# Gate and up products in four row tiles of TensorE: 27 groups of 32 rows in place of 7 passes of 128

## The chip, the core and the metric

One core of one Trainium2 chip runs the whole program. The metric is device time in microseconds from start to end of an execution, as the median of several executions. The profile is of one execution of the same program.

The engines have short names: PE is TensorE's matmuls, PEld its weight loads, DVE is VectorE, ACT is ScalarE, POOL is GpSimd and SP is SyncE, which issues most DMAs.

## What is computed

The input `x` is 2048 rows of 576. After a layer norm it goes through a linear attention block and through a gated feed-forward block; the output is `x + s * silu(f)`. The part that is changed is the first half of the feed-forward block:

```python
def _B_ref(x, w_gate, w_up, w_down):
    g = jnp.einsum("bsd,df->bsf", x, w_gate)     # 2048x576 by 576x4608
    u = jnp.einsum("bsd,df->bsf", x, w_up)       # 2048x576 by 576x4608
    h = _gelu(g) * u
    return jnp.einsum("bsf,fd->bsd", h, w_down)  # 2048x4608 by 4608x576
...
xn = _layernorm(x, axis=-1)
s = _A_ref(xn, A_wqkv, A_wo)
g = _silu(_B_ref(xn, B_w_gate, B_w_up, B_w_down))
return x + s * g
```

All is fp32.

## The kernel before

**Words.** TensorE's fast fp32 format (`F32R`) keeps fewer bits than fp32. Each operand is therefore cut in two: a high word (ScalarE copies it into the F32R type) and a low word (VectorE subtracts the high word from the source). A product of two operands is high times high plus high times low plus low times high.

**Seven products.** Gate and up are computed by Strassen's scheme in Winograd's form. The reduction of 576 is halved to 288, the 256 columns of a weight group are halved to 128, and blocks of 512 rows of x are taken in pairs. So one matrix (2 x 2 blocks of weights by 2 x 2 blocks of x) takes seven products of 128 by 288 by 512 in place of eight. The weight operands are A11, A12, A22 and the sums S1 to S4; those of x are B11, B21, B22 and the sums T1 to T4. There are 36 matrices, a gate and an up matrix for each of 18 groups of 256 columns (`NG`), and each handles both halves of the rows of x (`s` is 1, then 0), so there are 36 x 7 x 2 = 504 products. The x operands stay in SBUF for the whole stage; in the trace they are `xo_B`, `xo_T` (s = 1) and `xr_B`, `xr_T` (s = 0). The weight words are `wa` and `wb`.

**Passes.** The reduction of 288 is 2 x 128 + 32 rows. With two words on each side a product needs high-high, high-low and low-high: three times 288 is 864 rows, or 27 groups of 32. `PASSES` lays them out as seven matmuls of 128 rows: six for the two full pieces in three word combinations, and one pass that holds the three 32-row remainders in its row groups 0, 1 and 2, and zeros in group 3. `product` (line 801) issues them into one PSUM bank.

**Steps.** `matrix` runs seven steps, each for both s: A11 B11 into bank `al`, S2 T2 into `be`, S1 T1 into `ga`, S3 T3 into `de`, then A12 B21 on top of `al`, S4 B22 on top of `ga`, and A22 T4 on top of `de`. After each of the first four products an engine reads the bank: ScalarE copies `al` to `u`, VectorE adds `be` to `u`, then `ga` and `de` into the result for block (1, 1). After each of the last three, `done` takes the finished block: in a gate matrix ScalarE applies the gelu, in an up matrix VectorE multiplies the two and GpSimd (`L96`) makes the sums for the down projection. There are eight banks, one for each of `al`, `be`, `ga`, `de` and s. A bank's next writer waits until its reader is done.

**What else runs beside it.** `todo[k]` holds pieces of work that are put behind step k: `cut_w` cuts the weights of the next matrix into words (an ACTIVATE, then two VectorE subtractions, the second on the 32 rows of one row group), `mat_sums` forms S1 to S4 on GpSimd, `load_mat` and `load_down` issue loads on SP. Every engine runs its queue in the order of the program (`keep_in_program_order`). The stage is followed by the down projection (line 1007), 3024 matmuls of 288 columns.

Of the kernel before, what the change touches and what calls it, by code (L numbers as in the profile page):

```python
# [15 lines left out]
P = 128  # L16
# [32 lines left out]
PASSES = [(0, 0, P), (0, 3, P), (3, 0, P), (1, 1, P), (1, 4, P), (4, 1, P), (2, 2, P)]  # L49


X_SLOT = {"B11": 0, "B21": 1, "B22": 3, "T1": 9, "T3": 10, "T2": 11, "T4": 2}


@with_exitstack
def block_kernel(ctx, tc, x, xe, xt_d, wq_d, wkv0_d, wkv1_d, wkv2_d, wo, wgu_d, wd_d, out):
# [3 lines left out]
    ps = ctx.enter_context(tc.tile_pool(name="ps", bufs=1, space=PSUM))  # L60
    dr = ctx.enter_context(tc.tile_pool(name="dr", bufs=1, space=DRAM))

    def bank(name):
        return ps.tile([P, 512], F32, tag="one", bufs=6, name=name)

    def own_bank(name):
        return ps.tile([P, 512], F32, tag="own", bufs=2, name=name)

    def big(i, shape, dt, name):
        return sb.tile(shape, dt, tag=f"b{i}", bufs=1, name=name)  # L70
# [10 lines left out]
    def tmp(shape, name):  # L81
        return sb.tile(shape, F32, tag="tmp", bufs=4, name=name)
# [3 lines left out]
    def act(*args, **kw):  # L86
        pin(nc.scalar.activation(*args, **kw))  # L87

    def vec(op, *args, **kw):
        pin(getattr(nc.vector, op)(*args, **kw))  # L90

    def mm(*args, **kw):
        pin(nc.tensor.matmul(*args, **kw))  # L93

    def pool(op, *args, **kw):
        pin(getattr(nc.gpsimd, op)(*args, **kw))  # L96
# [118 lines left out]
    def place(n, js=(0, 1), words=(0, 1)):  # L215

        tb, t = divmod(n, TT)
        s, b = divmod(tb, 2)
        c = slice(t * P, (t + 1) * P)
        for j in js:  # L220
            nm = BS[b][j]
            if t == 0 and 0 in words:
                xo[s][nm] = big(2 * b + j, [P, 5, TBN], F32R, f"xo_{s}_{nm}")
            o, v = xo[s][nm], xts[n][j] if n < TT else xf[s][nm][:, :, c]
            if 0 in words:
                act(o[:, 0:3, c], v, AF.Copy)
            if 1 in words:
                vec("tensor_sub", o[:, 3:5, c], v[:, 0:2, :], o[:, 0:2, c].bitcast(F32))
                r = slice(KR, 2 * KR)
                vec("tensor_sub", o[r, 2, c], v[r, 2, :], o[r, 2, c].bitcast(F32))  # L230

    def save(n):
# [9 lines left out]

    mom, scale_of, xts, mr = {}, {}, {}, {}

    def to_operand(o, src, c):
        act(o[:, 0:3, c], src[:, :, c], AF.Copy)
        vec("tensor_sub", o[:, 3:5, c], src[:, 0:2, c], o[:, 0:2, c].bitcast(F32))
        vec("tensor_sub", 
            o[KR : 2 * KR, 2, c], src[KR : 2 * KR, 2, c], o[KR : 2 * KR, 2, c].bitcast(F32)
        )  # L250


    SUMS = (("T1", "B12", "B11", "B11"), ("T3", "B22", "B12", "B12"),
# [10 lines left out]
        dma(out=d, in_=o.bitcast(F32))  # L264
        store[s, nm] = d

    full = slice(0, TBN)

    def build(s, nm, i):
        xo[s][nm] = o = big(i, [P, 5, TBN], F32R, f"xo_{s}_{nm}")  # L270
        to_operand(o, xf[s][nm], full)
        return o


# [493 lines left out]
        pool("tensor_sub", sm[:, 3], a12, sm[:, 1])  # L768
        sums[q] = rv, sm

    def cut_w(o, src):

        r = slice(2 * KR, 3 * KR)
        act(o[:, :, 0:3, :], src, AF.Copy)
        vec("tensor_sub", o[:, :, 3:5, :], src[:, :, 0:2, :], o[:, :, 0:2, :].bitcast(F32))
        vec("tensor_sub", o[r, :, 2, :], src[r, :, 2, :], o[r, :, 2, :].bitcast(F32))

    def mat_pieces(q):

        if q >= NQ:  # L780
            return [[] for _ in range(7)]
        rv, sm = sums.pop(q)
        if q % 2 == 0:
            raws_ = [lambda: cut_w(wt["b"][:, 1:3], rv[:, 1])]
        else:
            raws_ = [
                lambda: cut_w(wt["b"][:, 1:2], rv[:, 1, 0:1]),
                lambda: cut_w(wt["b"][:, 0:1], rv[:, 1, 1:2]),
            ]
        return [  # L790
            [lambda: cut_w(wt["a"][:, 0:1], rv[:, 0, 0:1])],
            [], [],
            [lambda: cut_w(wt["a"][:, 1:4], sm[:, 0:3])],
            raws_,
            [lambda: cut_w(wt["b"][:, 3:4], sm[:, 3:4])],
            [],
        ]

    def product(o, w, xop, start):
        for n, (wi, xi, rows) in enumerate(PASSES):  # L800
            nc.tensor.matmul(  # L801
                o, w[0:rows, wi, :], xop[0:rows, xi, :],
                start=(start and n == 0), stop=(n == len(PASSES) - 1), skip_group_check=True,
            )

    def matrix(q, c22, done, todo):

        u, bs = {}, {}

        def both(bk, wn, xn, start):  # L810
            for s in SBS:
                if start:
                    bs[bk, s] = (own_bank if bk == "al" else bank)(f"{bk}_{q}_{s}")
                product(bs[bk, s], w_at(q, wn), X[s][xn], start)

        both("al", "A11", "B11", True)
        for s in SBS:
            u[s] = tmp([P, TBN], f"u_{q}_{s}")
            act(u[s], bs["al", s], AF.Copy)
        run(todo[0])  # L820
        both("be", "S2", "T2", True)
        for s in SBS:
            vec("tensor_add", u[s], u[s], bs["be", s])
        run(todo[1])
        both("ga", "S1", "T1", True)
        for s in SBS:
            vec("tensor_add", c22(s), u[s], bs["ga", s])
        run(todo[2])
        both("de", "S3", "T3", True)
        for s in SBS:  # L830
            vec("tensor_add", c22(s), c22(s), bs["de", s])
            done(s, 1, 1, None)
        run(todo[3])
        both("al", "A12", "B21", False)
        for s in SBS:
            done(s, 0, 0, bs["al", s])
        run(todo[4])
        both("ga", "S4", "B22", False)
        for s in SBS:
            done(s, 0, 1, (u[s], bs["ga", s]))  # L840
        run(todo[5])
        both("de", "A22", "T4", False)
        for s in SBS:
            done(s, 1, 0, (u[s], bs["de", s]))
        run(todo[6])

    hid = {}

    def gate_matrix(g, todo):
        for s in SBS:  # L850
            for b in range(2):
                hid[s, b] = slot([P, 2, TBN], F32, f"h_{g}_{s}_{b}")

        def done(s, f, b, src):
            o = hid[s, b][:, f]
            if src is None:
                src = o
# [5 lines left out]
        matrix(2 * g, lambda s: hid[s, 1][:, 1], done, todo)  # L863

# [7 lines left out]
    def up_matrix(g, todo):  # L872
        c22, sm = {}, {}

        def take(s):
            if s not in c22:
                c22[s] = tmp([P, TBN], f"u22_{g}_{s}")
            return c22[s]

        def done(s, f, b, src):  # L880
            if src is None:
                src = c22[s]
            elif isinstance(src, tuple):
# [22 lines left out]
        matrix(2 * g + 1, take, done, todo)  # L906

    td = {}

# [449 lines left out]
    run(pieces[4] + pieces[5])  # L1359
    load_mat(1)  # L1360
    back("B21", "B22", "T4", eng=nc.sync)
    for q in range(NQ):
        g = q // 2
        mat_sums(q + 1)
        todo = mat_pieces(q + 1)
        if q % 2 == 0:
            todo[0].append(lambda g=g: load_down(g))
            todo[3].append(lambda g=g: down_sums(g))
        todo[4].append(lambda q=q: load_mat(q + 2))
# [9 lines left out]
        (gate_matrix if q % 2 == 0 else up_matrix)(g, todo)  # L1379
    load_s(5)  # L1380
    down_all()

# [53 lines left out]
```

## Time and profile before

| | |
|---|---|
| time, median of 3 runs | 1490.42 us (1490.0 to 1490.95) |
| span of the profiled execution, first to last instruction | 1488.0 us |
| busy: PE, DVE, ACT, POOL | 1481.6, 1064.0, 563.5, 546.5 us |
| matmuls on line 801 (gate and up) | 3528, from 282.9 to about 1082.6 us |
| matmuls on line 1007 (down) | 3024, 401.0 us busy |
| granted TensorE clock | 1.000 |

For the profiled execution the profile gives the span; what lies around it is the difference to the time of a run, about 2.4 us. A row of the order of time reads: start, duration, engine, line, operation, written tile <- read tiles, shapes, and how many instructions were merged; in brackets, how long the engine had been idle and what ended that. A matmul's shape `128*128 128x512` is rows by columns of the weights, then partitions by columns of what is streamed. Ends of matmuls are modelled by the profile, starts are recorded.

### The profile page before, as it was taken

The page shows a single profiled execution, that of the slowest core. Times are in us where ns is not written, and L with a number is a line of the kernel's source. Part 1 is how long each engine was busy: PE and PEld are TensorE (multiplying, and loading weights), DVE is VectorE, ACT ScalarE, POOL GpSimd, SP SyncE. Part 2 cuts the span into 40 slices and gives each one's busy share as a digit, 9 for nine tenths or more (in the row PEclk, how much of TensorE's full clock was granted, in tenths as well). Part 3 has the DMA queues.
Part 4 walks back from the last instruction along what each step waited for, and adds up shares of the span by engine and source line. Part 5 has one row for each costly group of instructions (what it writes and reads, how often), then busy time and mean ns, then how long its engine had stood idle before and what let it go on. Part 6 is the DMA issues. An engine that isn't in the chain of part 4 may idle for free.

```text
span 1488.0 us, 22311 instructions
## 1 busy us (share of the span) xinstructions
PE 1481.6 (100%) x8351; PEld 1327.9 (89%) x8351; DVE 1064.0 (72%) x1579; ACT 563.5 (38%) x1047; POOL 546.5 (37%) x520
## 2 busy tenths in 40 slices
PE   9999999999999999999999999999999999999998
PEld 9989989988888888888888888888899999999998
DVE  7677567377778787788787778787785566555775
ACT  5444455332332222332223322223445454445443
POOL 5453431144565554565554565554310020000120
PEclk9999999999999999999999999999999999999999
DMA  6355015533344433344333344333697766786873
GB/s 239 131 213 181 1 46 192 228 147 133 147 173 158 152 118 121 145 174 166 143 128 124 133 173 174 136 140 113 221 332 254 233 213 223 227 288 223 299 248 119
DMA packets 114470, 260.67 MB, mean 175 GB/s; under 512 B 10218, under 2 KB 38634, under 8 KB 112314
## 3 DMA queue, kind: packets, MB, share of 16 engines
q1 hardware_dynamic: 112586, 249.95, 47.0%
q0 software_dynamic: 1632, 8.91, 1.6%
q8 instruction: 65, 1.06, 0.3%
q14 instruction: 43, 0.35, 0.1%
q10 hardware_dynamic: 144, 0.39, 0.1%
HBM read 161.27 MB, written 97.91 MB: 174 GB/s over the span
## 4 chain that ended last, share of the span: by engine, by line
PE 99%; DVE 0%; DMA 0%; ACT 0%; issue 0%; ACTq 0%
PE bd L1007 27%; PE al L801 15%; PE ga L801 15%; PE de L801 15%; PE kv L93 8%; PE be L801 8%; PE s L93 4%; PE q L93 3%; PE kv_a L93 1%; PE d L93 0%; PE kw L93 0%; PE b L93 0%; PE xt L213 0%; DMA x<-in_xe_dram 0%; PE mr L194 0%; PE kv_b L93 0%
## 5 line engine op out<-in xcount | busy, mean ns | idle before, releaser
L1007 PEld LDWEIGHTS bd<-t,s 128*128 128x128 f32 x3024 | 400.9, 188 | 0.1
L1007 PE MATMUL bd<-t,s 128*128 128x288 f32 x3024 | 401.0, 295 | 0.0
L90 DVE TENSOR_TENSOR s<-sr,s 128x512 fp32r<-128x512 f32 x252 | 176.2, 738 | 119.6 <-ACT s L87 115.2
L87 ACT ACTIVATE s<-sr 128x512 fp32r<-128x512 f32 x252 | 149.2, 625 | 189.5 <-PE bd L1007 134.6
L96 POOL TENSOR_TENSOR hs<-h,h 128x512 f32<-128x512 f32 x68 | 94.7, 1402 | 200.8 <-DVE h L90 198.2
L87 ACT ACTIVATE h<-h 128x512 f32<-128x512 f32 x108 | 67.0, 633 | 245.0 <-POOL sm L96 123.1
L96 POOL TENSOR_TENSOR sx<-sx 128x288 f32<-128x288 f32 x24 | 27.9, 1181 | 322.9 <-DVE sx L90 163.6
L93 PE MATMUL kv<-wkv,xo_B 128*128 128x416 f32 (+1 forms) x672 | 128.9, 348 | 0.0
L93 PEld LDWEIGHTS kv<-wkv,xo_B 128*128 128x128 f32 x672 | 121.6, 188 | 1.2 <-DVE xo_B L90 0.2
L96 POOL TENSOR_TENSOR sm<-raw 128x384 f32<-128x384 f32 x72 | 75.5, 1048 | 110.9 <-DMA raw<-in_wgu_dram 82.8
L90 DVE TENSOR_TENSOR wa<-raw,wa 128x256 fp32r<-128x256 f32 x72 | 79.4, 1102 | 51.3 <-ACT wa L87 48.0
L90 DVE TENSOR_TENSOR h<-h,u 128x512 f32<-128x512 f32 x108 | 95.7, 886 | 3.7
L87 ACT ACTIVATE wa<-sm 128x1152 fp32r<-128x1152 f32 x36 | 41.8, 1161 | 135.1 <-PE de L801 135.1
L90 DVE TENSOR_TENSOR wa<-sm,wa 128x768 fp32r<-128x768 f32 x72 | 63.1, 877 | 37.2 <-ACT wa L87 36.3
L96 POOL TENSOR_TENSOR td<-td 128x288 f32<-128x288 f32 x72 | 70.4, 978 | 52.1 <-DMA td<-in_wd_dram 47.9
L90 DVE TENSOR_TENSOR wb<-raw,wb 128x256 fp32r<-128x256 f32 (+1 forms) x108 | 71.8, 665 | 7.3 <-ACT wb L87 5.8
L90 DVE TENSOR_TENSOR wb<-sm,wb 128x256 fp32r<-128x256 f32 x72 | 61.5, 854 | 20.6 <-ACT wb L87 20.0
L87 ACT ACTIVATE u<-al 128x512 f32<-128x512 f32 x72 | 40.8, 592 | 88.4 <-PE al L801 88.4
L801 PE MATMUL al<-xo_B,wa 128*128 128x512 f32 x252 | 63.0, 389 | 0.0
L801 PE MATMUL al<-xr_B,wa 128*128 128x512 f32 x252 | 63.0, 389 | 0.0
L801 PE MATMUL be<-xo_T,wa 128*128 128x512 f32 x252 | 63.0, 389 | 0.0
L801 PE MATMUL be<-xr_T,wa 128*128 128x512 f32 x252 | 63.0, 389 | 0.0
(174 smaller groups left out, 2764.2 us busy)
## 6 DMA issues: line engine op xcount, KB each, us to landing
sr<-hs SPq DMA_DIRECT2D x252, 256.0 KB
hs<-h SPq DMA_DIRECT2D x68, 512.0 KB
raw<-in_wgu_dram SPq DMA_DIRECT2D x36, 768.0 KB
hs<-hs SPq DMA_DIRECT2D x102, 256.0 KB
td<-in_wd_dram SPq DMA_DIRECT2D x18, 576.0 KB
td<-td SPq DMA_DIRECT2D x18, 576.0 KB
tr<-td SPq DMA_DIRECT2D x16, 576.0 KB
tr<-in_wd_dram SPq DMA_DIRECT2D x12, 576.0 KB
```

The costliest lines, as they stand in the source:

```text
L87: pin(nc.scalar.activation(*args, **kw))
L90: pin(getattr(nc.vector, op)(*args, **kw))
L93: pin(nc.tensor.matmul(*args, **kw))
L96: pin(getattr(nc.gpsimd, op)(*args, **kw))
L801: nc.tensor.matmul(o, w[0:rows, wi, :], xop[0:rows, xi, :], start=(start and n == 0), stop=(n == len(PASSES) - 1), skip_group_check=True,)
L1007: nc.tensor.matmul(banks[j][:, 0:HALF], hw[n, s][:, a, t * P : (t + 1) * P], w[:, c, g % 4], start=(new and g == 0 and m == 0), stop=(g == ...
```

## The change

The reduction is no longer run in passes of 128 rows. TensorE is used as four row tiles of 32 rows and 128 columns each (`tile_position=(t * KR, 0)`), and each product is 27 matmuls of 32 rows: six or seven on every tile (the two full pieces in three word combinations, and a remainder on three of the four tiles). `roll` writes the whole stage as one list of steps; at each step every tile gets one matmul, in the order of tiles 0, 1, 2, 3. All four tiles add into the same bank for one product, but never at one time: tile t+1 starts a product after tile t has finished it, which a semaphore per tile (`tile_0` to `tile_2`) tells. So four products are under way, one on each tile. Which tile is left without a remainder (`empty`) is chosen to keep the four lists equally long.

The row groups of the remainders' words move to fit (`X_LO`, `W_LO`), and the remainder rows of the weights fill group 3 too, where zeros were. The banks get fixed places: `al` and `be` change places from one matrix to the next, `ga` and `de` keep theirs (`bank_of`). The work behind each step is the same and is issued where the step's last matmul stands in the list.

```diff
-    def product(o, w, xop, start):
-        for n, (wi, xi, rows) in enumerate(PASSES):
-            nc.tensor.matmul(
-                o, w[0:rows, wi, :], xop[0:rows, xi, :],
-                start=(start and n == 0), stop=(n == len(PASSES) - 1), skip_group_check=True,
-            )
+    STEPS = (
+        ("al", "A11", "B11"), ("be", "S2", "T2"), ("ga", "S1", "T1"), ("de", "S3", "T3"),
+        ("al", "A12", "B21"), ("ga", "S4", "B22"), ("de", "A22", "T4"),
+    )
+    def pairs_of(wn, xn, t, empty):
+        jobs = [(0, 0), (0, 3), (3, 0), (1, 1), (1, 4), (4, 1)]
+        return jobs if t == empty else jobs + [(2, 2)]
+    def bank_of(q, bk, s):
+        i = SBS.index(s)
+        if bk in ("al", "be"):
+            return i + (6 if (bk == "al") == (q % 2 == 0) else 0)
+        return i + (2 if bk == "ga" else 4)
+    def roll(matrix_of):
...
+        skew = [0]
+        for t in range(3):
+            skew.append(2 + skew[t] + max(
+                begins[t][p + 1] - begins[t + 1][p] for p in range(len(todo))))
...
+        for n in range(skew[3] + len(rows[3])):
+            for t in range(4):
+                i = n - skew[t]
+                if not 0 <= i < len(rows[t]):
+                    continue
...
+                i = mm(
+                    bs[q, bk, s], w_at(q, wn)[r, wi, :], X[s][xn][r, xi, :],
+                    start=(first and k < 4), stop=last, skip_group_check=True,
+                    tile_position=(t * KR, 0),
+                )
+                if t > 0 and j == 0:
+                    i._wait_ge(sems[t - 1], p + 1)
+                if t < 3 and j == len(jobs[t]) - 1:
+                    i.then_inc(sems[t])
...
+                if last:
+                    if k == 0 and s == SBS[0]:
+                        mats[q] = matrix_of(q)
+                    mats[q](k, s, bs[q, bk, s])
```

Here `begins[t][p]` is the place of product p in tile t's list, so `skew[t]` is the step at which tile t begins.

How this moves PE's instructions is seen at two places. The first is in gate matrix 18, from the product S1 T1 of s = 1 (operands `T1` and `wa`) to the next product into the same bank, S4 B22 (operands `B22` and `wb`). Before:

```order
L801 MATMUL ga_18_1_6123<-xo_1_T1_2329,wa_2921 128x512 x6
L801 MATMUL ga_18_0_6131<-xr_T1_2884,wa_2921 128x512 [waits DVE_49]
L801 MATMUL ga_18_0_6131<-xr_T1_2884,wa_2921 128x512 x6
L801 MATMUL de_18_1_6141<-xo_1_T3_2463,wa_2921 128x512 [waits DVE_49]
L801 MATMUL de_18_1_6141<-xo_1_T3_2463,wa_2921 128x512 x6
L801 MATMUL de_18_0_6149<-xr_T3_3031,wa_2921 128x512 [waits DVE_49]
L801 MATMUL de_18_0_6149<-xr_T3_3031,wa_2921 128x512 x6
L801 MATMUL al_18_1_6080<-xo_1_B21_1187,wb_3030 128x512 [waits Activation_49]
L801 MATMUL al_18_1_6080<-xo_1_B21_1187,wb_3030 128x512 x6
L801 MATMUL al_18_0_6088<-xr_B21_3041,wb_3030 128x512 [waits Activation_49]
L801 MATMUL al_18_0_6088<-xr_B21_3041,wb_3030 128x512 x6
L801 MATMUL ga_18_1_6123<-xo_1_B22_1521,wb_3030 128x512 [waits DVE_49]
```

The same place now, from the last matmul of S1 T1 (tile 3) on; all of the rows between are of four products under way:

```order
L110 MATMUL ga_18_1_11153<-xo_1_T1_2329,wa_2921 128x512
L110 MATMUL al_18_0_11039<-xr_B21_3041,wb_3030 128x512
L110 MATMUL al_18_1_11004<-xo_1_B21_1187,wb_3030 128x512 [waits tile_0]
L110 MATMUL de_18_1_11228<-xo_1_T3_2463,wa_2921 128x512
L110 MATMUL ga_18_0_11188<-xr_T1_2884,wa_2921 128x512 [waits tile_2]
...
L110 MATMUL de_18_1_11228<-xo_1_T3_2463,wa_2921 128x512
L110 MATMUL ga_18_0_11188<-xr_T1_2884,wa_2921 128x512
L110 MATMUL ga_18_1_11153<-xo_1_B22_1521,wb_3030 128x512 [waits DVE_49]
```

Five products of seven passes stood between the two; now 12 matmuls of 32 rows do, three steps of four tiles. The wait for VectorE, which reads the bank between the two, stays.

The second place is the passage from up matrix 19 to gate matrix 20, from the last product into `de` to the next matrix's first one. Before, the products between were:

```order
L801 MATMUL de_19_1_6298<-xo_1_T4_2676,wb_3030 128x512 x6
L801 MATMUL de_19_0_6306<-xr_T4_3045,wb_3030 128x512 [waits DVE_49]
...
L801 MATMUL ga_20_0_6467<-xr_T1_2884,wa_2921 128x512 [waits DVE_49]
L801 MATMUL ga_20_0_6467<-xr_T1_2884,wa_2921 128x512 x6
L801 MATMUL de_20_1_6477<-xo_1_T3_2463,wa_2921 128x512 [waits DVE_49]
```

Now the end of the one and the begin of the other read:

```order
L110 MATMUL de_19_1_11667<-xo_1_T4_2676,wb_3030 128x512
L110 MATMUL be_20_0_12014<-xr_T2_2680,wa_2921 128x512
...
L110 MATMUL be_20_1_11971<-xo_1_T2_2538,wa_2921 128x512
L110 MATMUL al_20_0_11935<-xr_B11_2588,wa_2921 128x512
L110 MATMUL de_20_1_12124<-xo_1_T3_2463,wa_2921 128x512 [waits DVE_49]
```

Seven products stood between; now 64 matmuls, 16 steps, do.

More of the change, by code (lines that the diff above doesn't have):

```diff
@@ L49, with group @@
 PASSES = [(0, 0, P), (0, 3, P), (3, 0, P), (1, 1, P), (1, 4, P), (4, 1, P), (2, 2, P)]
+X_LO = {"B11": 1, "B12": 1, "B21": 0, "B22": 0, "T1": 0, "T2": 1, "T3": 1, "T4": 1}
+W_LO = {"S1": 2, "S2": 2, "S3": 2, "S4": 3, "A11": 3, "A12": 3, "A22": 3}
+def group(t):
+    return slice(t * KR, (t + 1) * KR)
 X_SLOT = {"B11": 0, "B21": 1, "B22": 3, "T1": 9, "T3": 10, "T2": 11, "T4": 2}
@@ L61, in block_kernel, with bank_at @@
     dr = ctx.enter_context(tc.tile_pool(name="dr", bufs=1, space=DRAM))
+    turns = {"one": 0, "own": 0}
+    def bank_at(i, name):
+        return ps.tile([P, 512], F32, tag=f"bk{i}", bufs=1, name=name)
     def bank(name):
-        return ps.tile([P, 512], F32, tag="one", bufs=6, name=name)
+        turns["one"] += 1
+        return bank_at((turns["one"] - 1) % 6, name)
     def own_bank(name):
-        return ps.tile([P, 512], F32, tag="own", bufs=2, name=name)
+        turns["own"] += 1
+        return bank_at(6 + (turns["own"] - 1) % 2, name)
     def big(i, shape, dt, name):
@@ L92, in mm @@
     def mm(*args, **kw):
-        pin(nc.tensor.matmul(*args, **kw))
+        i = nc.tensor.matmul(*args, **kw)
+        pin(i)
+        return i
     def pool(op, *args, **kw):
@@ L769, in mat_sums, with cut_w @@
         sums[q] = rv, sm
[L771 to L773 removed]
+    def cut_w(o, src, nm):
+        r = group(W_LO[nm])
         act(o[:, :, 0:3, :], src, AF.Copy)
@@ L806, in matrix @@
-    def matrix(q, c22, done, todo):
[L808 to L845, printed above, removed]
@@ new lines, in matrix, with step @@
+    def matrix(q, c22, done, todo):
+        u = {}
+        def step(k, s, b):
+            if k == 0:
+                u[s] = tmp([P, TBN], f"u_{q}_{s}")
+                act(u[s], b, AF.Copy)
+            elif k == 1:
+                vec("tensor_add", u[s], u[s], b)
+            elif k == 2:
+                vec("tensor_add", c22(s), u[s], b)
+            elif k == 3:
+                vec("tensor_add", c22(s), c22(s), b)
+                done(s, 1, 1, None)
+            elif k == 4:
+                done(s, 0, 0, b)
+            elif k == 5:
+                done(s, 0, 1, (u[s], b))
+            else:
+                done(s, 1, 0, (u[s], b))
+            if s == SBS[-1]:
+                run(todo[k])
+        return step
@@ L904, in done @@
                 dma(out=d[:, 6], in_=sm[s][2], eng=eng)
-        matrix(2 * g + 1, take, done, todo)
+        return matrix(2 * g + 1, take, done, todo)
     td = {}
@@ L1361, in block_kernel, with matrix_of @@
     back("B21", "B22", "T4", eng=nc.sync)
-    for q in range(NQ):
+    def matrix_of(q):
         g = q // 2
@@ L1378, in block_kernel @@
             todo[6].append(lambda: prep_s(3))
-        (gate_matrix if q % 2 == 0 else up_matrix)(g, todo)
+        return (gate_matrix if q % 2 == 0 else up_matrix)(g, todo)
+    roll(matrix_of)
+    turns["one"] = 0
     load_s(5)
@@ L1387, with halves @@
     from concourse.bass_utils import run_bass_kernel_spmd
-    def halves(w):
+    def halves(w, full=False):
         w = w.reshape(2, HALF, -1)
         last = np.tile(w[:, 2 * P :], (1, P // KR, 1))
-        last[:, 3 * KR :] = 0
+        if not full:
+            last[:, 3 * KR :] = 0
         return np.stack([w[:, 0:P], w[:, P : 2 * P], last], axis=2)
```

67 lines of the change are left out of this document (47 added, 20 removed).

## The prediction

> **What bounds the kernel now.** I read the page first, then the busy time by stage, then the order of time inside one matrix, for TensorE, VectorE and ScalarE in turn.
>
> ```profile
> span 1488.0 us, 22311 instructions
> PE 1481.6 (100%) x8351; PEld 1327.9 (89%) x8351; DVE 1064.0 (72%) x1579; ACT 563.5 (38%) x1047; POOL 546.5 (37%) x520
> PE bd L1007 27%; PE al L801 15%; PE ga L801 15%; PE de L801 15%; PE kv L93 8%; PE be L801 8%; PE s L93 4%; PE q L93 3%; PE kv_a L93 1%; PE d L93 0%; PE kw L93 0%; PE b L93 0%; PE xt L213 0%; DMA x<-in_xe_dram 0%; PE mr L194 0%; PE kv_b L93 0%
> ...
> 266.00:1066.00 800.00, 800.00 (x3584) 665.56 (x3583) 613.92 (x814) 232.68 (x390) 409.70 (x350) 1.00 0.41 152
> ```
>
> The chain is matmuls from end to end, and 53% of it is line L801, the gate and up products. The last row (PE, PEld, DVE, ACT and POOL busy in this stretch, then clock and DMA) holds nearly all of that stage: PE is never idle, at the full clock (1.00), and VectorE is busy 77%. A microsecond won or lost by PE there is one in the time.
>
> ```profile
> 600.05 1.55 PEld L801 LDWEIGHTS ga<-xo_T,wa 128*128 128x128 f32 x7
> 600.27 1.75 PE L801 MATMUL ga<-xo_T,wa 128*128 128x512 f32 x7
> 601.86 1.75 PE L801 MATMUL ga<-xr_T,wa 128*128 128x512 f32 x7
> 603.45 1.75 PE L801 MATMUL de<-xo_T,wa 128*128 128x512 f32 x7
> 605.03 1.30 PE L801 MATMUL de<-xr_T,wa 128*128 128x512 f32 x5
> ...
> L801 PEld LDWEIGHTS ga<-xo_T,wa x252: 187/188/188, 289.1 to 1067.9; 128*128 128x128 f32 x126
> L801 PE MATMUL ga<-xo_T,wa x252: 389/389/389, 289.3 to 1068.1; 128*128 128x512 f32 x126
> ```
>
> Products begin every (605.03 - 600.27) / 3 = 1.587 us, so a pass every 0.2267 us, and a matmul ends 0.389 after it starts. 504 products of 7 passes are 3528 x 0.2267 = 799.8 us.
>
> **The passes.** 27 groups of 32 rows for each of 504 products are 13,608 matmuls, dealt to four tiles: 3401, 3402, 3402 and 3403. Each tile starts a product 10 steps after the tile before it (two steps of room and up to 8 of unequal shares), so the loop has 3403 + 30 = 3433 steps. If the four run side by side and a step keeps its 0.2267 us, that is 778.3 us: a gain of **21.5 us**. The 30 steps of filling and draining are in it.
>
> Row tiles do not occur in this trace. The nearest rows are the four column tiles of the denominators, 32 columns each:
>
> ```profile
> 202.77 1.03 PEld L93 LDWEIGHTS d<-ph,small 128*32 128x32 f32 x40 [0.35 <-issue]
> 202.77 1.30 PE L93 MATMUL d<-ph,small 128*32 128x128 f32 x40
> ...
> 161.65 1.04 PE L93 MATMUL kv_a<-pk,va 128*127 128x126 f32 x8
> ...
> L93 PE MATMUL kv_a<-pk,va 128*127 128x126 f32 x128 | 16.7, 273 | 0.0
> L93 PEld LDWEIGHTS d<-ph,small 128*32 128x32 f32 x160 | 4.1, 110 | 0.8 <-issue 0.8
> ```
>
> Forty tiled matmuls take 1.30 us, (1.30 - 0.273) / 39 = 0.026 each. Untiled ones of nearly the same length start every (1.04 - 0.273) / 7 = 0.109 us. So four tiles, their loads included, run in the time of one. I carry that to row tiles: cost per step 0 as likeliest, with two other prices among the rivals. The same rows show 80 instructions issued in 1.30 us, 0.016 each; a step here has eight, 0.13 of its 0.2267 us, so issue is hidden. It would be the bound from 0.028 on.
>
> PE's program grows by 20,160 instructions.
>
> ```profile
> q8 instruction: 65, 1.06, 0.3%
> ```
>
> The columns are packets, MB and share. A packet is 16 KB, 256 instructions at 64 bytes (1.41 MB in both instruction queues for 22,311 recorded), and took 0.003 x 16 x 1488 / 65 = 1.1 us; PE uses 256 in 32 steps, 7.3 us. Hidden behind the matmuls themselves.
>
> **The waits between tiles.** A tile waits until the one before it has finished the product; 1512 such waits. At the narrowest there are 2 free steps, so 0.680 us from the last matmul's start to the next one's. It needs 0.389, a semaphore and a fresh load (0.20 together, from the rows below): 0.59. Cost 0, with 0.09 to spare.
>
> **The reuse of the banks.** This is what I expect to decide. A product now lasts about 37 steps from its first matmul to its last instead of 7, because it passes through the tiles in turn. Bank `ga` is written by S1 T1, read by VectorE, and written again by S4 B22 six products later; `de` likewise by S3 T3 and A22 T4. Before, five whole products (7.9 us) lay between. Now, as the order above shows, 3 free steps do, or 4: over the loop's own lists the two occur equally often. From the start of the last matmul to that of the next writer there are 4 or 5 steps: 0.907 or 1.133 us. What has to fit:
>
> ```profile
> 599.25 2.80 DVE L90 TENSOR_TENSOR wa<-raw,wa 128x256 fp32r<-128x256 f32 x2
> 602.09 1.28 DVE L90 TENSOR_TENSOR u<-u,be 128x512 f32<-128x512 f32 x2
> 603.29 1.28 DVE L90 TENSOR_TENSOR h<-u,ga 128x512 f32<-128x512 f32 x2
> 605.23 0.69 DVE L90 TENSOR_TENSOR h<-h,de 128x512 f32<-128x512 f32 x1 [0.66 <-PE de L801]
> 606.00 0.63 ACT L87 ACTIVATE h<-h 128x512 f32<-128x512 f32 x1 [7.70 <-POOL sm L96]
> ...
> 204.00 0.99 PEld L93 LDWEIGHTS q<-xo_B,wq 128*128 128x128 f32 x5 [0.20 <-issue]
> 204.00 1.42 PE L93 MATMUL q<-xo_B,wq 128*128 128x512 f32 x5
> ```
>
> The `de` product of 603.45 ends at 605.20, and its sum ends at 605.92: 0.72 later. ScalarE, which waits for that sum, starts 0.08 after it. A PE that starts from rest pays 1.42 - 4 x 0.2267 - 0.389 = 0.12 for the load that it could not do ahead. Together 0.389 + 0.72 + 0.08 + 0.12 = 1.31 us: PE stands 0.40 or 0.18, 0.29 in the mean. PE's queue is in order and the waiting matmul is tile 0's, so the other three stand behind it; nothing covers this. Four such waits in each of 36 matrices: 144 x 0.29 = **42 us**.
>
> VectorE is often late. In the rows above the `ga` product of 600.27 ends at 602.02, but its sum, the first of two at 603.29, ends only at about 603.95, 1.93 later, since the cut of the next weights (599.25, 2.80 us) and the two `be` sums stand ahead of it in the same queue. That is 1.21 over the simple case, once in each gate matrix: 18 x 1.21 = **22 us**. The second `ga` sum is 0.96 late, but the stall before it gives that back.
>
> ```profile
> 609.79 1.75 PE L801 MATMUL ga<-xo_B,wb 128*128 128x512 f32 x7
> 614.47 1.29 DVE L90 TENSOR_TENSOR h<-u,ga 128x512 f32<-128x512 f32 x2
> ...
> 635.18 1.75 PE L801 MATMUL de<-xo_T,wb 128*128 128x512 f32 x7
> 636.76 1.75 PE L801 MATMUL de<-xr_T,wb 128*128 128x512 f32 x7
> ...
> 637.56 2.80 DVE L90 TENSOR_TENSOR wb<-sm,wb 128x256 fp32r<-128x256 f32 x2
> 640.39 0.69 DVE L90 TENSOR_TENSOR u<-u,de 128x512 f32<-128x512 f32 x1
> 641.99 0.68 DVE L90 TENSOR_TENSOR u<-u,de 128x512 f32<-128x512 f32 x1
> ```
>
> The first two rows are the worst case inside a gate matrix: S4 B22 ends at 611.54, its sum near 615.1, 3.6 late. At the end of an up matrix the `de` sums end 641.08 - 636.93 = 4.15 us late, behind the cut of S4. The next writer of that bank comes 15 or 16 free steps later, 3.63 or 3.85 us after the last start, where 0.389 + 4.15 + 0.20 = 4.74 are wanted: 0.9 to 1.1 short. The simple stalls just before let VectorE catch up by about half, so 0.5 x 18 = **9 us**.
>
> `al` (8 products apart, read by ScalarE) and `be` (12 apart) have room. The cuts write weights that a product still reads for 30 steps (6.8 us) longer, and each has over 20 free steps left until its use. VectorE, ScalarE, GpSimd and the DMA queues issue the same instructions in the same order, with the same sizes.
>
> **Sum.** -21.5 + 42 + 22 + 9 = +51.5 us on the span of 1488.0: 1539.5. The median of 1490.42 is 2.4 us over that span, for what lies around it: **1542 us**. Its own range: with every simple stall at 0.18 and no backlog, 26 us, 1495; with all delays as they stand before and nothing given back (42 + 22, and per pair of matrices 0.24, twice 1.1, and 0.7, twice 0.389 + 3.6 + 0.20 less 3.85, for the gate's last two products), 121 us, 1590.
>
> **Rivals.**
> Free banks: the reads come in time. For it: VectorE has 23% idle, and a matmul's end is modelled, so 0.389 may be too long. Against: 0.69 of the 1.31 is one VectorE instruction. It gives 1490.4 - 21.5 = 1469 and ends on the other side of no change; it decides once all stalls sum to less than 21.5 us, 0.15 for each of the 144.
>
> A longer step: four streams read weights, read rows and write four banks at once, and share some port. Nothing in the trace speaks for it except that no row tile is there. Each tenth is 78 us, while longer steps ease the waits: at a tenth 56 + 54 of stalls, 1600; at a fifth 134 + 38, about 1660. The Trainium skill has four row tiles at 3.07 times the speed of one, not four (TensorE: Matmul & The Clock Gate, "Measured speedup vs the span model"). By that figure a step would be 4 / 3.07 = 1.30 of 0.2267, an estimate of 1490 + 234 = 1724 us before any stall; no run here has shown it, and the column tiles above show the full four.
>
> One loader: the four loads of a step pass one after another. Against it, the 40 loads of `d` take 1.03 us though each lasts 0.110. A load of 127 columns fits in 0.109 (`kv_a`), so a step would be 0.436 and the stage 1497: about 2187 us. It decides from 0.057 a load. The Trainium skill says that a load's time goes by its columns and that 32 rows take as long as 128 (same page, "LDWEIGHTS"): by that rule quarter-height loads are no cheaper, and nothing is gained if they queue.
>
> No side by side at all: 13,608 x 0.2267 = 3085 us, a time near 3775.
>
> **Numbers.** Forecast 0.66, longer step 0.15, free banks 0.08, one loader 0.07, none side by side 0.04. The range 1480 to 1660 holds the forecast, two thirds of the longer steps and a part of the free banks: 0.8. A measurement tells from no change what is over 0.2%, 3 us: faster 0.07, same 0.03, slower 0.90.
>
> **What would show it.** In the trace of after: matmuls of the four tiles starting within some 0.03 us of each other and every 0.227 us; PE idle for 0.2 to 0.4 us ahead of the S4 B22 and A22 T4 products and up to 1.6 ahead of the gate's first, put down to VectorE; the gate and up stage about 850 us long. A step well off 0.227, or no idle ahead of those products, makes the forecast wrong.

## The result, and the profile after

| | before | changed |
|---|---|---|
| time, median | 1490.45 us (1490.0 to 1490.95) | 1549.15 us (1548.65 to 1549.95) |
| ratio, 95% interval | | 1.0395 (1.0381 to 1.041) |
| span of the profiled execution | 1488.0 us | 1547.8 us |
| first to last matmul start of the gate and up stage | 799.5 us | 854.7 us |

The changed kernel is 58.7 us slower. The forecast was 1542 us, in a range of 1480 to 1660. The page after begins so, and its chain reads:

```profile
span 1547.8 us, 42471 instructions
PE 1506.8 (97%) x18431; PEld 1360.0 (88%) x18431; DVE 1044.2 (67%) x1579; ACT 566.5 (37%) x1047; POOL 544.4 (35%) x520
q8 instruction: 144, 2.36, 0.6%
PE bd L1072 26%; PE de L110 1%; PE ga L110 1%; PE al L110 0%; DVE wa L107 0%; DVE h L107 0%; DVE u L107 0%; PE be L110 0%; DVE sx L107 0%; ACT u_d L104 0%; DVEq L107 0%
```

Gate and up now come from line 110 and the down projection from line 1072. PE's busy time is 41 us below the span, where it was 6 below. The chain, matmuls almost alone before, now passes through VectorE's `h`, `u` and `wa`. (With four tiles at once its shares no longer add up to the span, and how much of the time it holds can't be read from them.) Instruction packets have grown from 65 to 144, and no idle time of the stage is put down to them.

Cut at the stage's borders, the busy times are (time, length, PE, PEld, DVE, ACT, POOL, clock, DMA share, GB/s; ahead of the stage, the stage, behind it):

```profile
0.00:284.40 284.40, 280.90 (x1800) 264.55 (x1800) 183.76 (x380) 138.72 (x340) 103.51 (x138) 1.00 0.39 142
284.40:1139.40 855.00, 821.89 (x13609) 691.98 (x13608) 608.94 (x828) 237.75 (x391) 408.75 (x351) 1.00 0.40 144
1139.40:1547.80 408.40, 403.96 (x3025) 403.45 (x3024) 251.54 (x372) 190.01 (x316) 32.15 (x32) 0.99 0.72 241
```

Of the 59.8 us by which the span has grown, 55.3 are in the stage (854.7 for 799.5), 1.5 ahead of it (it begins at 284.4, before at 282.9) and 3.0 behind it. PE stands for 33 us in the stage, and its loads for more, as the list of what they waited for tells (total, times, longest):

```profile
PEld ga L110 <- DVE h L107: 33.1, 36, 1.3
PEld de L110 <- DVE u L107: 29.5, 53, 1.1
PEld ga L110 <- DVE u L107: 15.9, 36, 0.6
PEld de L110 <- DVE h L107: 15.8, 36, 0.6
```

Apart from one of 0.2 us, these are the banks `ga` and `de` and nothing else, and VectorE is the one they wait for: 161 waits, the 144 of the prediction and 17 between an up matrix and the next gate matrix. The 94 us are idle time of the loads, a part of which lies under the previous step's matmuls. What a wait costs is read from the starts of the matmuls. One plain wait, that is one with no long work of VectorE ahead of the read, inside an up matrix (VectorE's row, then rows of the four tiles in the order of time):

```profile
656.28 0.69 DVE L107 TENSOR_TENSOR u<-u,de 128x512 f32<-128x512 f32 x1 [1.10 <-PE de L110]
...
655.80 0.39 PE L110 MATMUL de<-xo_T,wa 32*128 32x512 f32 x1
656.03 0.39 PE L110 MATMUL ga<-xr_B,wb 32*128 32x512 f32 x1
656.03 0.39 PE L110 MATMUL ga<-xo_B,wb 32*128 32x512 f32 x1
656.03 0.39 PE L110 MATMUL al<-xo_B,wb 32*128 32x512 f32 x1
656.04 0.39 PE L110 MATMUL de<-xr_T,wa 32*128 32x512 f32 x1
...
656.72 0.38 PE L110 MATMUL ga<-xr_B,wb 32*128 32x512 f32 x1
...
657.02 0.49 PE L110 MATMUL de<-xo_T,wb 32*128 32x512 f32 x1
...
657.36 0.39 PE L110 MATMUL de<-xo_T,wb 32*128 32x512 f32 x1
```

The last matmul of S3 T3 starts at 655.80 and lasts 0.385; VectorE begins 0.10 after its end and is done at 656.97; the next matmul into that bank starts 0.05 later, at 657.02, instead of 656.95. The step after it comes 0.34 later instead of 0.23, because the load of a step that has just been released can't lie under the matmuls before it (the four loads and the four matmuls are all recorded at 657.02). So this wait, with four free steps, costs 0.07 + 0.11 = 0.18 us, and the way from the last matmul's start to the next writer's, restart included, is 1.22 + 0.11 = 1.33 us.

The rows of 656.03 show the other half of the change: the four tiles start within 0.01 us of each other. Their loads do too, although each takes 0.18 (a load of 128 rows took 0.19 before):

```profile
656.03 0.18 PEld L110 LDWEIGHTS ga<-xr_B,wb 32*128 32x128 f32 x1
656.04 0.18 PEld L110 LDWEIGHTS ga<-xo_B,wb 32*128 32x128 f32 x1
656.04 0.18 PEld L110 LDWEIGHTS al<-xo_B,wb 32*128 32x128 f32 x1
656.04 0.18 PEld L110 LDWEIGHTS de<-xr_T,wa 32*128 32x128 f32 x1
```

The long waits have a queue behind them. At the end of an up matrix and at the beginning of the next gate matrix:

```profile
619.43 2.81 DVE L107 TENSOR_TENSOR wb<-sm,wb 128x256 fp32r<-128x256 f32 x2
622.27 0.69 DVE L107 TENSOR_TENSOR u<-u,de 128x512 f32<-128x512 f32 x1
...
625.55 2.81 DVE L107 TENSOR_TENSOR wa<-raw,wa 128x256 fp32r<-128x256 f32 x2
628.39 1.29 DVE L107 TENSOR_TENSOR u<-u,be 128x512 f32<-128x512 f32 x2
629.59 0.68 DVE L107 TENSOR_TENSOR h<-u,ga 128x512 f32<-128x512 f32 x1
...
623.01 0.18 PEld L110 LDWEIGHTS de<-xo_T,wa 32*128 32x128 f32 x1 [1.04 <-DVE u L107]
630.33 0.18 PEld L110 LDWEIGHTS ga<-xo_B,wb 32*128 32x128 f32 x1 [1.26 <-DVE h L107]
```

The read of `de` stands behind the cut of S4 (619.43, 2.81 us), and PE restarts 0.05 after it. The read of `ga` stands behind the cut of A11 (625.55, 2.81 us) and two `be` sums. The same waits come back in each pair of matrices.

### The profile page after: what moved, and what is told of

Its sections match the earlier page's. It is cut to its first block, busy times and chain, and to the rows that moved or that the text cites. A ratio compares the mean times of both kernels' runs of the same rounds, so it can differ in the third digit from the quotient of the medians.

```text
span 1547.8 us, 42471 instructions
## 1 busy us (share of the span) xinstructions
PE 1506.8 (97%) x18431; PEld 1360.0 (88%) x18431; DVE 1044.2 (67%) x1579; ACT 566.5 (37%) x1047; POOL 544.4 (35%) x520
## 5 line engine op out<-in xcount | busy, mean ns | idle before, releaser
L110 PE MATMUL ga<-xo_B,wb 32*128 32x512 f32 x972 | 258.1, 397 | 17.2 <-DVE h L107 14.6
L110 PE MATMUL de<-xo_T,wa 32*128 32x512 f32 x972 | 259.1, 394 | 10.6 <-DVE u L107 10.6
L110 PE MATMUL al<-xo_B,wb 32*128 32x512 f32 x972 | 265.4, 397 | 0.0
L110 PE MATMUL al<-xr_B,wb 32*128 32x512 f32 x972 | 262.2, 397 | 0.0
L110 PE MATMUL ga<-xr_B,wb 32*128 32x512 f32 x972 | 257.0, 395 | 3.2 <-DVE h L107 3.1
L110 PE MATMUL de<-xr_T,wa 32*128 32x512 f32 x972 | 258.8, 395 | 0.0
L110 PE MATMUL ga<-xr_T,wa 32*128 32x512 f32 x972 | 253.7, 390 | 0.0
L110 PE MATMUL de<-xr_T,wb 32*128 32x512 f32 x972 | 248.5, 390 | 2.2
L110 PE MATMUL de<-xo_T,wb 32*128 32x512 f32 x972 | 248.7, 390 | 0.0
L110 PE MATMUL ga<-xo_T,wa 32*128 32x512 f32 x972 | 248.3, 387 | 0.0
```

The costliest lines, as they stand in the source:

```text
L110: i = nc.tensor.matmul(*args, **kw)
```

## The experiments

Each is the changed kernel with one edit; of a longer edit the lines that matter are shown. Times are compared with the kernel before on the same chip.

**One step of room more or less (e4, e5).** `skew` gives each tile's handover two steps of room; each step taken away brings the writers of a bank three steps further behind its reader's product.

```diff
-            skew.append(2 + skew[t] + max(
+            skew.append(1 + skew[t] + max(    # e5: 3 +
```

Expected of one step, then of three:

> The change, with one step of room between tiles in place of two. A product takes 3 steps (0.68 us) less. Theory A: plain waits need 1.31 us and now have 1.59 or more, so 44 us go and the backlog ones shrink to about 0.7 us a pair; at the narrowest hand-overs 0.45 us now stand against 0.59 needed, 143 places at 0.13 to 0.24: 1510 to 1525 us. Theory B: hand-overs get tighter and nothing is won, 1549 us or more.

> The change, with three steps of room between tiles in place of two. A product takes 3 steps (0.68 us) more. Theory A: each of the 144 waits for a reader grows by 0.68 us, 98 us, and waits between matrices that just fitted appear, 15 to 35 us: 1660 to 1685 us. Theory B: three steps more in the whole stage, 0.7 us: 1550 us.

With one step it took 1503.76 us, ratio 1.0089 (1.0069 to 1.0109), 45 us less than the changed kernel and 6 under the lower end of what was expected. With three it took 1650.83, 1.1076 (1.1054 to 1.1098), 9 under the lower end. The loads' waits with one step:

```profile
PEld ga L110 <- DVE h L107: 22.1, 17, 1.3
PEld de L110 <- DVE u L107: 5.5, 18, 0.8
```

The plain waits are gone; the gate's first (17 x 1.08 us) and a remainder of the passage between matrices (17 x 0.23) stay, each with 0.11 of restart. Here it was better than expected for one reason and worse for another. The waits behind VectorE's backlog did not shrink to 0.7 us a pair of matrices, they are 1.53. But the handovers cost next to nothing. The expectation had counted 0.59 us as needed for one, and one free step is 0.45 from start to start. What happens is that the tiles shift against each other:

```profile
699.67 0.38 PE L110 MATMUL de<-xo_T,wa 32*128 32x512 f32 x1
699.70 0.38 PE L110 MATMUL al<-xr_B,wb 32*128 32x512 f32 x1
699.71 0.38 PE L110 MATMUL al<-xo_B,wb 32*128 32x512 f32 x1
699.72 0.38 PE L110 MATMUL ga<-xr_T,wa 32*128 32x512 f32 x1
```

Here tiles 1 to 3 are 0.03 to 0.05 us behind tile 0. A wait for VectorE brings the tiles back to within some 0.01 (as at 701.20 us, 1.5 us after these rows), and then the shift grows again, up to some 0.23. The median offsets of tiles 1 to 3 are 0.015, 0.097 and 0.154 us (0.005, 0.011 and 0.022 in the changed kernel), at 0.228 a step all the same.

The plain waits follow the free steps between a bank's read and its writer: practically none with one step of room, 0.18 to 0.47 us with two, 0.85 to 1.16 with three. That is the theory of the prediction. The gate's first wait does not follow them: 1.19, 1.13 and 1.23 us with restart, while the passage just ahead of it goes from 0.34 to 0.92 and 1.59. This fits a backlog of VectorE that is worked off in one of the two places or the other; that it is so was not tested by itself.

**VectorE's long cuts (e2).** Is the length of the gate's first wait the cut in front of the sum? From matrix 2 on, VectorE's two subtractions of every weight cut are left out, so the low words are those of earlier weights and the output is no longer the block's; only the time is of use.

```diff
+        sums_done.append(q)
...
+        if len(sums_done) > 2:
+            return
```

> The change, with VectorE's two subtractions of each weight cut left out from matrix 2 on (low words stay those of earlier matrices). Theory A: the two waits that come from VectorE's backlog lose what exceeds a plain wait, 1.13 - 0.40 and 0.92 us a pair of matrices, 18 x 1.65 = 30 us: about 1519 us, with the plain waits of 0.18 to 0.47 us left as they are. Theory B: no change, 1549 us.

It took 1521.13 us, 1.0206 (1.0185 to 1.0226), 2 above what was expected. Without the restart, the gate's first wait falls from 1.02 to 0.39 us, which is a plain wait; the passage between matrices has none left, and the plain ones are unchanged. All cuts were left out at once; which of them stands in front of which sum is read from the rows above.

**The four first sums apart (e1, then e8, e7 and e9).** The order of the products is changed so that the two uses of `ga`, of `de` and of `al` are four or more products apart, the second partial sum is gathered in a buffer `v` that ScalarE fills, and the pairs of banks turn from matrix to matrix.

```diff
-        ("al", "A11", "B11"), ("be", "S2", "T2"), ("ga", "S1", "T1"), ("de", "S3", "T3"),
+        ("al", "A11", "B11"), ("ga", "S1", "T1"), ("de", "S3", "T3"), ("be", "S2", "T2"),
...
+        k = ("al", "ga", "de", "be").index(bk)
+        return SBS.index(s) + 2 * ((NS * q + k) % 4)
...
+                v[s] = tmp([P, TBN], f"v_{q}_{s}")
+                act(v[s], b, AF.Copy)
```

> Row tiles as in the change, but the steps run in the order al, ga, de, be, al, ga, de over four pairs of banks in turn, so every bank is written again 8 products after its last writer and not 6 (ScalarE copies ga aside, VectorE makes as many sums as before). Theory A, the reader between two writers of a bank is too late: some 16 free steps, 3.8 us, stand where 3 or 4 did; the 0.2 to 0.4 us waits at S4 B22 and A22 T4 go (44 us), and what is left are waits behind the weight cuts, 20 to 45 us: 1495 to 1525 us. Theory B, row tiles themselves cost the time (handing a product on, restarting the tiles): as many steps and hand-overs as in the change, so about 1549 us.

It took 1534.79 us, 1.0305 (1.0287 to 1.0322): 14 less than the changed kernel, and 10 more than the upper end of what was expected. The plain waits at S4 B22 and A22 T4 are gone. But the turned banks put other products behind VectorE's cuts:

```profile
PEld be L110 <- DVE u L107: 41.1, 34, 2.1
PEld de L110 <- DVE h L107: 17.4, 17, 1.6
```

S2 T2 of a gate matrix now waits for a read of `de` that stands behind the cut of S4 (17 x 1.88 us), S3 T3 of an up matrix behind the cut of the raw weights (17 x 0.80), and 35 shorter waits of S2 T2 cost some 0.18 each. With the room of one step as well (e8):

> Four apart with one step of room, no cut moved. Theory A: the two waits left in the run four apart (1.88 and 0.80 us a pair) lose 0.68 us each, some 23 us: 1512 us. Theory B: room does not matter once the banks are four apart, 1535 us.

1519.1 us, 1.0202 (1.0186 to 1.0218), 7 above theory A; S2 T2 still waits 17 x 1.33 us and S3 T3 17 x 0.32. In front of the read that S2 T2 waits for stands the cut of S4. It can go behind the last step (e7), since its weights are needed only at the sixth step of the next matrix:

```diff
-            [lambda: cut_w(wt["b"][:, 3:4], sm[:, 3:4], "S4")],
             [],
+            [lambda: cut_w(wt["b"][:, 3:4], sm[:, 3:4], "S4")],
```

> Four apart, one step of room, and of the weight cuts only S4's put later, behind step 6; the raw cuts and the load of the next raw weights stay behind step 4. Theory A: in the run four apart the waits left were 33 us at S2 T2 of the gate, behind the S4 cut of the up matrix, and 14 us at S3 T3 of the up matrix, behind the raw cuts; the first goes with the move, the second shrinks by the 0.68 us of room: 2 to 10 us left, a stage of 785 to 790 us and 1479 to 1485 us. Theory B (the two late runs were slow because VectorE has no time left, not because the load was late): 1510 us or more.

1487.15 us, 0.9979 (0.997 to 0.9987): 3 us, or 0.2%, under the kernel before, and 2 above what was expected. Nearly the whole stage, on the same columns as above:

```profile
286.00:1063.00 777.00, 777.00 (x13553) 764.42 (x13554) 603.91 (x811) 274.10 (x456) 416.11 (x348) 1.00 0.43 157
```

PE has no idle time in it. The stage runs 784.3 us from first to last start, 15.2 less than before; so with the waits gone the four tiles do bring most of the 21.5 us. Of these 15.2, 2.0 are lost ahead of the stage (it begins at 284.9) and 9.3 behind it:

```profile
1067.84 1.74 PE L110 MATMUL de<-xr_T,wb 32*128 32x512 f32 x7
1069.51 0.79 PE L1072 MATMUL bd<-t,s 128*128 128x288 f32 x4
1077.16 13.01 PE L1072 MATMUL bd<-t,s 128*128 128x288 f32 x81 [6.85 <-DVE u L107]
```

The last `de` lies in the two banks that the down projection fills first, and VectorE has read the first of the two only at 1077.10; PE goes on 0.06 later. Turning the banks by one pair (e9, `(NS * q + k + 3) % 4`) should have removed that:

> The run four apart with S4 late, with the four pairs of banks turned by one place, so that the last product of the stage (A22 T4) lies in banks 4 and 5 and not in 6 and 7, which the down projection fills first. Theory A (what is left is one wait of 6.9 us of the down projection's first matmuls for VectorE's last reads of those banks): 1480 us, 0.7% under the kernel before. Theory B (VectorE's queue is as late for any bank there): 1487 us.

It did not: 1487.26 us, 0.998 (0.9971 to 0.999). The one wait had become three:

```profile
PEld bd L1072 <- DVE u L107: 5.7, 3, 3.1
```

VectorE has the sums of the last products and the words of the first down operands to make at that place. With the banks turned PE stands 4.9 us for it in three places, where it stood 6.9 in one, and the time is the same; other places of the banks were not tried.

**Weight work later (e3, e6).** Two attempts moved more of `todo`: e3 is e8 with the cut of the raw weights, the cut of S4 and the loads of the matrix after next each one step later, so it is e7 with the raw cut and the loads later; e6 keeps the changed kernel's order of products, with room of one step, A11's cut behind step 3, and the cuts of A12, A22 and S4 and the loads behind step 6. Of the edits the line of the loads is shown:

```diff
-        todo[4].append(lambda: load_mat(q + 2))
+        todo[5].append(lambda: load_mat(q + 2))    # e6: todo[6]
```

Expected of e3, then of e6:

> Four apart as before, with one step of room, and two weight cuts put later in VectorE's queue: the raw ones (A12, A22) behind step 5 and S4 behind step 6, with the load of the next raw weights behind step 5. Theory A (only readers held up behind cuts were left): all waits of the stage go, 3430 steps of 0.2276 us = 781 us against 799.7 before, and 4.4 us come back before and after the stage as in the change: 1476 us, up to 1485 if a wait is left. Theory B (VectorE, some 92% used in an up matrix, is the next bound, or other cuts come too late for the first tile): 1490 us or more.

> The change's own order of steps and its banks, one step of room, and the cuts moved so that none stands ahead of the reads of ga and de: A11 behind step 3, A12, A22 and S4 behind step 6, the load of the next raw weights there too. Theory A: the 20 us at S4 B22 of the gate and the 6 us between matrices that one step of room left go: 1476 to 1482 us. Against it: A11's words are then ready only about when tile 0 wants them, some 7 us later than before, so PE may wait for VectorE or GpSimd's sums there instead, up to 1 us in each matrix, 36 us: 1512 us.

Both made it slower: 1583.58 us, 1.0629 (1.0602 to 1.0656), and 1568.76, 1.0521 (1.0507 to 1.0535). The waits of e3:

```profile
POOL sm L115 <- DMA raw<-in_wgu_dram: 198.2, 35, 11.0
ACT wa L104 <- DMA raw<-in_wgu_dram: 137.0, 34, 8.1
PEld ga L110 <- ACT v L104: 58.3, 17, 4.3
```

In the changed kernel GpSimd waits 70.8 us for these loads, 11 times; ScalarE isn't seen waiting for them. The load overwrites the buffer that the cut reads, so it is issued behind the cut, and a cut one step later makes it a step later. ScalarE's queue is in order: its copies of `ga` stand behind the cut that waits for the load, and PE stands behind the copies.

```profile
636.42 0.52 ACT L104 ACTIVATE wa<-raw 128x384 fp32r<-128x384 f32 x1 [7.04 <-DMA raw<-in_wgu_dram]
636.85 1.07 ACT L104 ACTIVATE v<-ga 128x512 f32<-128x512 f32 x2
...
637.48 0.18 PEld L110 LDWEIGHTS ga<-xo_B,wb 32*128 32x128 f32 x1 [3.29 <-ACT v L104]
```

That is 3.2 us in each pair of matrices, 54 us. In e6 GpSimd waits 295.9 us for the same loads, and PE for `wa` of both ScalarE and VectorE: the words themselves are late. Its largest waits are still the gate's first, 17 x 1.64 us: the cuts of A12, A22 and S4, moved behind the last step of an up matrix, now stand right ahead of the `be` and `ga` sums of the next gate matrix (5.9 us of VectorE's queue from 628.09 on). Neither tells how far the cuts alone could have been moved.

**The clock behind the stage (e10, e11).** In the changed kernel the first matmuls of the down projection start every 0.24 us, not every 0.133 as before. The granted clock (last but two) is the reason:

```profile
1132.00:1138.80 6.80, 6.80 (x67) 5.82 (x61) 6.49 (x11) 2.31 (x4) 1.11 (x2) 1.00 0.64 215
1138.80:1145.60 6.80, 6.80 (x28) 6.15 (x26) 6.53 (x11) 0.00 (x0) 2.69 (x5) 0.50 0.82 300
1145.60:1152.40 6.80, 6.80 (x53) 6.80 (x53) 6.80 (x11) 2.06 (x4) 1.60 (x3) 1.00 1.02 367
```

Ahead of it lies the drain of the tiles: two of them from about 1134.3, one from 1136.7 on. Is that the cause, and is it what costs the 3 us? The drain was filled with matmuls that nobody reads, on the tiles that have run out; in e11 so was that of e7, with 28 full matmuls (6.7 us) between the last product and the down projection.

```diff
+                if i >= len(rows[t]):
...
+                    mm(
+                        fill[t], w_at(NQ - 1, "A22")[r, 0, :], X[SBS[0]]["T4"][r, 0, :],
+                        start=True, stop=True, skip_group_check=True, tile_position=(t * KR, 0),
+                    )
```

Expected of e10, then of e11:

> The changed kernel, with one addition: in the last 30 steps, when tiles 0, 1 and 2 run out of products one after the other, each goes on with a matmul of 32 rows whose result nobody reads (60 in all, at the same time as the work of the other tiles, so that they cost nothing by themselves). Theory A: the granted clock falls to 0.5 for 6.8 us at the end of the stage because TensorE's work had thinned out to two tiles and one. Then the stretch at 0.5 is gone, the first matmuls of the down projection start every 0.133 us, and the time is 2.7 us less than the changed kernel's 1549.15: 1546.5. Theory B: the clock falls for something that the change to the down projection brings (its operands, its transfers). Then the stretch stays, and the time is 1549.

> The version with the four first sums apart, room of one step and only the cut of S4 late (1487.15 us), with the drain filled in the same way and 28 more matmuls of 128 rows that nobody reads between the last product and the down projection (6.4 us, inside the 7.15 us in which TensorE waits for VectorE there). Theory A: without the 10.2 us at a clock of 0.5 (4.4 us of them lie under running matmuls, of which half is lost) 2.2 us are saved: 1485.0. Theory B: the stretch stays, 1487.

The clock stays through the drain, the time doesn't follow. The window behind the filled drain, and the start of the down projection, of e10:

```profile
1138.80:1142.20 3.40, 3.30 (x60) 2.79 (x52) 3.26 (x6) 1.15 (x2) 1.12 (x2) 1.00 0.28 111
1142.20:1145.60 3.40, 2.81 (x19) 2.62 (x20) 3.26 (x6) 0.00 (x0) 1.09 (x2) 1.00 0.84 306
...
1142.25 2.60 PE L1082 MATMUL bd<-t,s 128*128 128x288 f32 x18
1145.39 0.66 PE L1082 MATMUL bd<-t,s 128*128 128x288 f32 x3 [0.54 <-DVE u L107]
1147.44 4.85 PE L1082 MATMUL bd<-t,s 128*128 128x288 f32 x23 [1.39 <-DVE u L107]
```

At the full clock PE runs into VectorE's reads: 0.54 and 1.39 us of idle time that the changed kernel, at the half clock, does not have, and after them a mean clock of 0.84 and 0.65 in the next two stretches. e10 took 1549.36 us, 1.0399 (1.0385 to 1.0413), no change from 1549.15. The profiled execution is its slowest, 1553.36 us (the others took 1548.11 to 1549.76): there the clock is also 0.50 from 287.8 to 294.6, at the beginning of the stage, where the tiles start one after the other and nothing was filled; 51 matmuls start in that stretch, and 102 at the full clock in the changed kernel. The executions of one kernel say the same of the time: one of the changed kernel's four has a mean clock of 1.000 and took 1548.65 us, three have 0.998 and took 1548.79 to 1549.95; of e4's two, 1.000 goes with 1503.81 and 0.998 with 1503.71. e11 shows a clock of 1.00 in each stretch around its border and took 1486.45 us, 0.9974 (0.9963 to 0.9985): the lowest of all here, 3.6 us under the kernel before, but its 0.7 under e7 is less than these measurements tell apart. So theory A holds for the clock and not for the time. Theory B has the time, but not for its reason: VectorE, 96% busy there (3.26 of 3.40), releases the banks no earlier.

## Why the prediction was right, step by step

- **The passes, -21.5 us.** Right in kind: four tiles run side by side, with starts within 0.01 to 0.02 us. A step that follows no wait takes 0.2277 us, not 0.2267; over 3433 steps that is 3.4 us, so the gain is 18.1. The Trainium skill's 3.07 for four row tiles (TensorE: Matmul & The Clock Gate, "Measured speedup vs the span model") doesn't hold for this stream: 4 x 0.2267 / 0.2277 is 3.98. (The prediction's own estimate by that figure should read about 1703 us, not 1724: it leaves out the 21.5 us that it takes off in the other sums.) The rivals of a longer step, of one loader (the loads at 656.03 run at one time) and of no side by side fall with it.
- **The plain waits, 42 us.** Measured 0.18 with four free steps and 0.41 to 0.47 with three (predicted 0.18 and 0.40). There are eight kinds (gate or up, `ga` or `de`, s 1 or 0). With the gate's first counted at 0.44, as its like in the up matrix, they sum to 2.49 us for a pair of matrices, 18 x 2.49 = 44.8. Its parts were right too: VectorE 0.10 after the product instead of 0.03, PE 0.05 after VectorE instead of 0.08, restart 0.11 instead of 0.12. e4 and e5 show that the free steps set them.
- **The gate's first sum, 22 us.** The place and the cause were right (VectorE's cuts by e2, A11's by the rows), the size was not: 1.13 instead of 1.61 a wait, so 18 x 0.69 = 12.4 over the plain one. The backlog was carried over from before unshortened; yet at 622 to 624, just ahead, PE had already stood for VectorE. That this takes from the next backlog fits e4 and e5, but was not tested alone.
- **Between matrices, 9 us.** Measured 0.81 + 0.11 in each of 17, 15.6. Here the half given back was too much: nearly all of the 0.9 to 1.1 remained. (There are 17 such places, not 18.)
- Together 44.8 + 12.4 + 15.6 = 72.8 where 73 stood: one term was 10 too high, the other two 3 and 7 too low, and that they cancel is luck. With -18.1 that would be 54.7, and the stage grew by 55.3.
- **Not foreseen** are the 1.5 us ahead of the stage and the 3.0 behind it. The first lie in the first 25 us of the program: PE is idle for 3.5 us ahead of the stage instead of 2.0, and four gaps of 0.28 to 0.55 us, which the profile puts down to VectorE, make up the difference. Why VectorE is later there stays open. The second is the half clock, or VectorE's reads where the clock stays. With the 3.4 of the longer step they make up 7.9 of the 8.3 us between the forecast span of 1539.5 and 1547.8.
- **Instructions and the waits between tiles, 0.** Right: none of the stage's waits is put down to instruction loading or to another tile. That a handover needs 0.59 us was a little too much: in e4 the narrowest have 0.45 us and the shift of one tile against the one before it, 0.015 to 0.082 in the median, so 0.47 to 0.54, and that is enough.
- **Free banks, 1469.** The rival was nearly the right account of what the stage is worth without waits: e7's comes to 784.3 where 778.3 was forecast, though with another order of products and 11 us lost around it. In the changed kernel it did not happen because the 161 waits were there.

## What to carry to other kernels

Handing a product from tile to tile keeps the multiplier full but makes each product live several times as long, and with the same number of banks the gap between a bank's reader and its next writer shrinks by as much: here from five products (7.9 us) to three or four free steps (0.9 or 1.1 us from start to start), less than the 1.33 us that a read with restart takes. Count that gap in steps before choosing the interleaving, take the smallest skew that runs (one step here gave back 45 of 59 us), and put the reader of a bank ahead of long work in its engine's queue. Moving that work later paid here where no load was issued behind it (S4's cut, e7); where the load moved along (e3, e6) it cost more than it saved.

## What the runs showed of the hardware

- The granted clock can halve in a thin stretch in which PE is never idle: in the changed kernel it is 0.50 for 6.8 us (28 matmuls where 53 start at the full clock) after some 4.5 us in which two tiles and then one of 32 rows worked, and in e10 for 6.8 us from 287.8 on, where the tiles start one after the other. It does not do so each time: the changed kernel's profile has 1.00 at that beginning, and one of its four executions has a mean clock of 1.000. With the drain filled on all four tiles the clock stays at 1.00 up to 1145.6 us in e10, and in all of the profiled stage of e11 (two of e11's seven executions have a mean of 0.997 and 0.998; all eleven of e7, without the filling, lie at 0.992 to 0.997). The Trainium skill tells of a half rate after an idle window of about 3.4 us (TensorE: Matmul & The Clock Gate, Part 1). In the thin stretches there was no idle window; in e3, 17 idle times of PE of 3.0 us in the mean, 3.9 at most, went with 13 stretches of half clock inside the stage. How little work counts as idle, these runs do not show.
- Four loads of different row groups run at one time: four of 0.18 us start within 0.01 us of each other (656.03 in the changed kernel).
- Row tiles need not start together. With one step of room (e4) tile 3 starts 0.154 us behind tile 0 in the median, in e7 0.212, and a step without waits still takes 0.228 us. So a handover that is a little too short for its wait cost next to nothing there.
